# Issuing the wo loads of a layernorm, linear-attention and GEGLU block before the xn transposes

## The chip, the cores and the metric

The kernel runs on one core of a Trainium2 chip. The metric is device time in microseconds (us), the median of three runs. The profile is one further execution, read by engine: PE (matmuls; PEld is its weight load), ACT, DVE, POOL, and SP, which here only issues DMAs.

## The reference

One sequence of 2048 tokens, width 448, 16 heads of 28, hidden width 1792, all bf16.

```python
x = A_x
h = x + A(layernorm(x), wqkv, wo)
out = h + B(layernorm(h), w_gate, w_up, w_down)

# A: q, k, v = split(x @ wqkv);  phi(t) = where(t > 0, t + 1, exp(t)) + 1e-6
#    kv = phi(k)^T v;  z = sum(phi(k));  o = phi(q) kv / (phi(q) z + 1e-6);  return o @ wo
# B: (gelu(x @ w_gate) * (x @ w_up)) @ w_down
```

## The kernel before

The 2048 tokens are 16 tiles of 128. Three stages overlap. In the first, each tile of x is loaded, its statistics are taken (`bnst`, `bnag`), it is normalised into `xn` (`norm`), and it is transposed into `xnT`, so that the width lies on the partitions. Tiles 0 to 3 are transposed on PE (`tr0` to `tr3`). Tiles 4 to 15 are transposed by DMA: `xT4` to `xT15`, each a DMA_TRANSPOSE that SP issues (L526), once POOL has written `xn` of the tile and ACT has copied the last 64 columns beside it (`dup`). PE then computes K and V of each tile (`k4`, `v4` and so on: 14 matmuls from `xnT`, in two halves) and adds phi(K)^T V into two PSUM banks (`acc`). Q comes in four chunks of 512 tokens (`qa`, `qb`).

In the second stage PE forms numerator and denominator (`nd`), o is transposed (tiles 0 and 1 on PE, the others by `oT` DMA transposes), and `wo0` to `wo14b` multiply by `wo_sb`. In the third, h is normalised and transposed (`hT`), PE runs gate and up (`gu0` to `gu55`, from `wgu_sb`), ACT the gelu, DVE the product, and `down` multiplies by `wd_sb`.

The order on every engine is written out by hand: `ORDERS` holds one string of task names for each of PE, ACT, DVE, POOL and SP, and each engine runs its tasks strictly in that order, waiting on semaphores for what a task reads. A wait in SP's string therefore holds back every DMA behind it. All loads are issued by SP except the K and V weights, which ACT issues at the start.

`wo_sb` is filled by four DMAs: `dwo` and `dwo_s` of 128 x 3 rows of 448 elements (336 KB each), and `dwo_t` and `dwo_u` of 64 rows (56 KB each). They write parts of `wo_sb` that nothing else writes, and they read only the input. Three names near them matter below: `dwq`, `dwq_t`, `dwq_u` load the Q weights into `wq_sb`, `pqones` writes a 16 KB row of ones into `pqT`, and `dwg0` to `dwu6` load the gate and up weights into `wgu_sb` (14 DMAs of 224 KB).

Of the kernel before, what the change touches and what calls it, by code (L numbers as in the profile page):

```python
# [61 lines left out]
)  # L62
# [168 lines left out]
def bass_sequential_preLN__linear_attn_block__glu_gated_geglu__prompt_kernel(  # L231
    nc, A_x, A_wqkv, A_wo, B_x, B_w_gate, B_w_up, B_w_down, out, cfg=None
):
    cfg = dict(cfg or {})
    S, D, FF = 2048, 448, 1792
# [25 lines left out]
    with es:  # L261
        block = es.enter_context(nc.Block())

        def sb(name, shape, dt):
            return es.enter_context(nc.sbuf_tensor(name, shape, dt))
# [7 lines left out]
        wo_sb = sb("wo_sb", [128, 7, D], BF16)  # L273
# [41 lines left out]
        def bufs(name, n):  # L315
            return [_Buf("%s%d" % (name, i)) for i in range(n)]
# [4 lines left out]
        b_wk, b_wv, b_wq, b_wo = _Buf("wk"), _Buf("wv"), bufs("wq", 4), bufs("wo", 4)  # L321
# [38 lines left out]
        def dma(out_ap, in_ap, w, name, nbytes, q="sp", key=None, r=(), after=(), first=False):  # L360
            ik[0] += 0.01
            if first:
                after = chain[q][-1:]
            t_ = G.add(q, lambda e: e.dma_start(out_ap, in_ap), r=r, w=w, name=name, kind="dma", key=ik[0] if key is None else key, nbytes=nbytes, after=after)
            if first:
                chain[q].append(t_)
            return t_

        def op(eng, fn, r, w, name, dur, key=None, after=()):
            if key is None:  # L370
                ik[0] += 0.01
                key = ik[0]
            return G.add(eng, fn, r=r, w=w, name=name, dur=dur, key=key, after=after)
# [18 lines left out]
        dma(wq_sb[:, 0:3, 0:D], krows(A_wqkv, 0, 384, 0, D), [b_wq[0]], "dwq", 384 * D * 2, first=True)  # L392
        dma(wq_sb[0:64, 3, 0:D], A_wqkv[384:448, 0:D], [b_wq[1]], "dwq_t", 64 * D * 2, first=True)
        dma(wq_sb[64:128, 3, 0:D], A_wqkv[384:448, 0:D], [b_wq[2]], "dwq_u", 64 * D * 2, first=True)
        op("pool", lambda e: e.memset(ones_bf[:], 1.0), [], [b_ones], "ones", 0.20)  # L395
        op("pool", lambda e: e.affine_select(ident[:], ones_bf[:], [[1, 128]], ALU.is_equal, 0.0, base=0, channel_multiplier=-1),
           [b_ones], [b_ident], "ident", 0.30)
# [131 lines left out]
        wg3 = B_w_gate.rearrange("(k p) n -> p k n", p=64)  # L529
        wu3 = B_w_up.rearrange("(k p) n -> p k n", p=64)  # L530
        prev = xts[-1:]
        prev = [dma(wo_sb[:, 0:3, :], A_wo[0:384, :].rearrange("(g p) n -> p g n", p=128), [b_wo[0]], "dwo", 384 * D * 2, after=prev, key=19.0)]
        prev = [dma(wo_sb[0:64, 3, :], A_wo[384:448, :], [b_wo[1]], "dwo_t", 64 * D * 2, after=prev, key=19.0)]
        prev = [dma(wo_sb[64:128, 3, :], A_wo[0:64, :], [b_wo[2]], "dwo_u", 64 * D * 2, after=prev, key=19.0)]
        prev = [dma(wo_sb[:, 4:7, :], A_wo[64:448, :].rearrange("(g p) n -> p g n", p=128), [b_wo[3]], "dwo_s", 384 * D * 2, after=prev, key=19.0)]
        for k in range(7):
            prev = [dma(wgu_sb[0:64, k, :], wg3[:, k, :], [b_wg[k]], "dwg%d" % k, 64 * FF * 2, after=prev, key=20.0)]
            prev = [dma(wgu_sb[64:128, k, :], wu3[:, k, :], [b_wu[k]], "dwu%d" % k, 64 * FF * 2, after=prev, key=20.0)]
# [374 lines left out]
```

## Time and profile before

| | us |
|---|---|
| median of 3 runs | 196.42 (196.16 to 196.70) |
| profiled execution, its time | 196.7 |
| its span, first to last instruction | 194.9 |
| PE busy | 190.3 (98%) |
| PEld, DVE, ACT, POOL busy | 137.9, 116.3, 78.2, 42.0 |
| DMA traffic | 17.53 MB, mean 90 GB/s |

A row of the timeline reads: start, duration, engine, source line, operation, what is written and read, and how many. For a DMA on SP the duration is that of the issue; the time to landing stands in the list of DMA issues. Line 430 is a helper that issues most matmuls, and line 364 is the helper of all plain DMAs, so their rows are told apart by the tiles that they name. The span is 1.8 us shorter than the time of the same execution.

### The profile page before, as it was taken

How to read it: one execution, taken by the hardware profiler on the slowest of the kernel's cores; microseconds unless marked ns; L12 is line 12 of the kernel's file. 1: busy time of each engine (PE TensorE's matmuls, PEld its weight loads, DVE VectorE, ACT ScalarE, POOL GpSimd, SP SyncE). 2: the span in 40 equal slices, each digit the busy share in tenths (PEclk: the TensorE clock that was granted, in tenths of full speed). 3: DMA queues.
4: the chain of work that ended last, by engine and by line, in shares of the span. 5: the costliest groups of instructions: out<-in, count | busy, mean ns of one | idle time of the engine just before them, and what ended most of it. 6: DMA issues, size and time to landing. Idle time of an engine off the chain costs nothing.

```text
span 194.9 us, 5336 instructions
## 1 busy us (share of the span) xinstructions
PE 190.3 (98%) x2192; PEld 137.9 (71%) x2192; DVE 116.3 (60%) x301; ACT 78.2 (40%) x205; POOL 42.0 (22%) x90
## 2 busy tenths in 40 slices
PE   7999999999999999999999999999999999999994
PEld 7556658754588977976675577877778779899554
DVE  2989735368998946843967745756735443431512
ACT  3689866669784212220442441233232442411100
POOL 3099974300050310500500500500500000000000
PEclk9999999999999999999999999999999999999999
DMA  6944558999836052152062250172040000010111
GB/s 191 377 116 97 81 110 185 247 248 205 260 103 110 15 101 50 50 105 62 10 129 46 46 106 2 30 117 51 5 94 28 23 0 0 3 47 3 47 47 47
DMA packets 37256, 17.53 MB, mean 90 GB/s; under 512 B 28272, under 2 KB 36336, under 8 KB 37232
## 3 DMA queue, kind: packets, MB, share of 16 engines
q1 hardware_dynamic: 36352, 16.45, 36.8%
q10 hardware_dynamic: 880, 0.75, 1.2%
q8 instruction: 17, 0.28, 0.6%
q14 instruction: 7, 0.06, 0.1%
HBM read 8.72 MB, written 1.84 MB: 54 GB/s over the span
## 4 chain that ended last, share of the span: by engine, by line
PE 96%; issue 1%; ACT 1%; DVE 1%; POOL 0%; DVEq 0%; ACTq 0%; POOLq 0%
PE ps L430 87%; PE ps L780 6%; PE ps L454 2%; DVE x_sb L660 1%; PE ps L495 1%; ACT xn L617 1%; PE ps L681 0%; ACT xnT L523 0%; PE ps L672 0%; DVE x_sb L756 0%; POOL ones_bf L395 0%; POOL eps_t L398 0%; ACT pqT L616 0%; DVEq L196 0%; ACTq L196 0%
## 5 line engine op out<-in xcount | busy, mean ns | idle before, releaser
L430 PE MATMUL ps<-hnT,wgu_sb 64*128 64x512 bf16 (+1 forms) x980 | 90.4, 333 | 0.0
L430 PEld LDWEIGHTS ps<-hnT,wgu_sb 64*128 64x128 bf16 x980 | 64.5, 94 | 18.6 <-DVE hh L832 1.7
L830 ACT ACTIVATE gl<-ps 128x256 bf16<-128x256 f32 x112 | 36.9, 381 | 89.3 <-PE ps L430 88.2
L832 DVE TENSOR_TENSOR hh<-ps,gl 128x256 bf16<-128x256 f32 x112 | 42.5, 415 | 35.7 <-ACT gl L830 31.5
L430 PE MATMUL ps<-wd_sb,hh 64*128 64x448 bf16 x336 | 34.4, 349 | 0.0
L430 PEld LDWEIGHTS ps<-wd_sb,hh 64*128 64x128 bf16 x336 | 25.6, 94 | 6.2 <-DVE x_sb L756 0.2
L430 PE MATMUL ps<-wkv_sb,xnT 64*128 64x448 bf16 x192 | 22.4, 350 | 0.4 <-ACT xnT L523 0.4
L462 DVE BATCH_NORM_STATS2 st<-x_sb 128x6 f32<-128x448 bf16 x32 | 18.7, 611 | 2.6 <-DMA x_sb<-in_A_x_dram 2.6
L756 DVE TENSOR_TENSOR x_sb<-ps,x_sb 128x448 bf16<-128x448 f32 (+1 forms) x17 | 9.9, 591 | 16.6 <-PE ps L430 9.8
L474 POOL TENSOR_SCALAR ln<-mv 128x2 f32<-128x2 f32 x7 | 1.6, 223 | 75.0 <-DVE mv L463 74.9
L568 DVE SCALAR_TENSOR_TENSOR pk<-ps,tm 128x448 bf16<-128x448 f32 x16 | 9.8, 620 | 9.6 <-POOL tm L566 7.1
L430 PE MATMUL ps<-xnT,wq_sb 64*128 64x512 bf16 x112 | 14.9, 377 | 0.2 <-ACT xn L617 0.2
L430 PEld LDWEIGHTS ps<-wkv_sb,xnT 64*128 64x128 bf16 x192 | 10.1, 94 | 6.3 <-issue 0.8
L430 PE MATMUL ps<-wo_sb,oT 64*128 64x448 bf16 x98 | 12.1, 350 | 0.1
L660 DVE TENSOR_TENSOR x_sb<-ps,x_sb 128x448 bf16<-128x448 f32 x16 | 9.4, 618 | 4.6 <-PE ps L430 4.4
L780 PE MATMUL ps<-wd_sb,hh 128*128 128x448 bf16 (+1 forms) x70 | 10.8, 315 | 0.0
L566 POOL TENSOR_SCALAR tm<-e 128x448 bf16<-128x448 bf16 x16 | 8.9, 559 | 6.4 <-ACT e L565 5.5
L487 POOL TENSOR_SCALAR hn<-x_sb,nm,rs 128x448 bf16<-128x448 bf16 x14 | 10.0, 720 | 0.8 <-POOL rs L476 0.2
L565 ACT ACTIVATE e<-ps 128x448 bf16<-128x448 f32 x16 | 8.5, 541 | 3.5 <-PE ps L430 2.2
L780 PEld LDWEIGHTS ps<-wd_sb,hh 128*128 128x128 bf16 x70 | 6.7, 98 | 4.3 <-issue 0.4
L655 DVE TENSOR_TENSOR o_sb<-ps,rd 128x448 bf16<-128x448 f32 x16 | 9.4, 612 | 0.1
L570 ACT ACTIVATE v<-ps 128x448 bf16<-128x448 f32 x16 | 8.4, 542 | 2.1 <-PE ps L430 2.1
(69 smaller groups left out, 140.4 us busy)
## 6 DMA issues: line engine op xcount, KB each, us to landing
out_dram<-x_sb SPq DMA_DIRECT2D x15, 112.0 KB, 1.7
wgu_sb<-in_B_w_gate_dram SPq DMA_DIRECT2D x7, 224.0 KB, 6.1
wgu_sb<-in_B_w_up_dram SPq DMA_DIRECT2D x7, 224.0 KB, 6.4
wd_sb<-in_B_w_down_dram SPq DMA_DIRECT2D x1, 1568.0 KB, 8.3
x_sb<-in_A_x_dram SPq DMA_DIRECT2D x2, 448.0 KB, 5.3
wkv_sb<-in_A_wqkv_dram ACTq DMA_DIRECT2D x2, 336.0 KB, 3.7
x_sb<-in_A_x_dram SPq DMA_DIRECT2D x3, 224.0 KB, 4.2
wo_sb<-in_A_wo_dram SPq DMA_DIRECT2D x2, 336.0 KB, 4.4
```

The lines of the kernel that those rows point to most:

```text
L430: ins = e.matmul(o_, l_, r_, start=s_, stop=p_, **kw)
L462: op("dve", lambda e: e.bn_stats(st[:, t, :], src_ap), [b_src], [b_st[t]], "%sbnst%d" % ("" if mv is mv1 else "h", t), 0.53, key, after=after)
L487: return lambda e: e.tensor_scalar(dst, src[:, t, :], nm[:, t:t + 1], rs[:, t:t + 1], ALU.add, ALU.mult)
L565: act_exp(lambda e: e.activation(e1[:, ie, :], oK, AF.Exp), bank(bk), [b_e1[ie]], "ek%d" % t, _c_act(D), kk)
L566: op("pool", lambda e: e.tensor_scalar(tm1[:, ie, :], e1[:, ie, :], 1.0 + EPS, 0.0, ALU.min, ALU.max), [b_e1[ie]], [b_tm1[ie]], "cl%d" % t ...
L568: op("dve", lambda e: e.scalar_tensor_tensor(pk[:, i, :, 0:GW], psK3, EPS, tm1[:, ie, :].rearrange("p (g e) -> p g e", g=NG), ALU.max, ALU ...
L655: op("dve", lambda e: e.tensor_tensor(o_sb[:, so, oc:oc + D].rearrange("p (a e) -> p a e", e=28), nd3[:, :, 0:28], rd[:, i, :].unsqueeze(2 ...
L660: op("dve", lambda e: e.tensor_tensor(h_sb[:, u, :], ps[:, b, 0:D], x_sb[:, u, :], ALU.add), bank(b) + [b_x[u]], [b_h[u]], "hr%d" % u, 0.5 ...
L756: op("dve", lambda e: e.tensor_tensor(x_sb[:, t, c0:c1], ps[:, bk, c0:c1], h_sb[:, t, c0:c1], ALU.add), bank(bk) + [b_h[t]], [bo], "out%d% ...
L780: ins = e.matmul(ps[:, bk, c0:c1], hh[:, j, hsl(t)], wd_sb[:, j, c0:c1], start=(j == 0), stop=(j == NJ - 1))
L830: G.add("act", lambda e, gi=gi, cs_=cs_, psG=psG: e.activation(gl[:, gi, cs_], psG[:, cs_], AF.Gelu_apprx_tanh), r=bank(BK_G[i]), w=[b_glh ...
L832: op("dve", lambda e, dst=dst, srcU=srcU, srcL=srcL: e.tensor_tensor(dst, srcU, srcL, ALU.mult), bank(BK_U[i]) + [b_glh], [b_ar[j_][t % HR ...
```

## The change

The four wo loads move in SP's order from behind `xT15` to behind `dwq_u`, ahead of `pqones` and of `xT4`. They are chained to the first loads instead of to the transposes. No other engine's order changes.

```diff
-    "dx0 dx1 dx2 dwv_t dx4 dx6 dx8 dx12 dwq dwq_t dwq_u pqones xT4 xT5 ... xT15"
-    " dwo dwo_t dwo_u dwo_s dwg0 dwu0 ...
+    "dx0 dx1 dx2 dwv_t dx4 dx6 dx8 dx12 dwq dwq_t dwq_u dwo dwo_t dwo_u dwo_s pqones xT4 xT5 ... xT15"
+    " dwg0 dwu0 ...
...
         dma(wq_sb[64:128, 3, 0:D], A_wqkv[384:448, 0:D], [b_wq[2]], "dwq_u", 64 * D * 2, first=True)
+        dma(wo_sb[:, 0:3, :], A_wo[0:384, :].rearrange("(g p) n -> p g n", p=128), [b_wo[0]], "dwo", 384 * D * 2, first=True)
+        dma(wo_sb[0:64, 3, :], A_wo[384:448, :], [b_wo[1]], "dwo_t", 64 * D * 2, first=True)
+        dma(wo_sb[64:128, 3, :], A_wo[0:64, :], [b_wo[2]], "dwo_u", 64 * D * 2, first=True)
+        dma(wo_sb[:, 4:7, :], A_wo[64:448, :].rearrange("(g p) n -> p g n", p=128), [b_wo[3]], "dwo_s", 384 * D * 2, first=True)
...
         prev = xts[-1:]
-        prev = [dma(wo_sb[:, 0:3, :], ..., "dwo", 384 * D * 2, after=prev, key=19.0)]
-        prev = [dma(wo_sb[0:64, 3, :], ..., "dwo_t", 64 * D * 2, after=prev, key=19.0)]
-        prev = [dma(wo_sb[64:128, 3, :], ..., "dwo_u", 64 * D * 2, after=prev, key=19.0)]
-        prev = [dma(wo_sb[:, 4:7, :], ..., "dwo_s", 384 * D * 2, after=prev, key=19.0)]
```

On SP, from the Q weights to the first gate weights, the program before reads as follows (`wq_sb` are the Q weights, `pqT` the ones, `xnT` the twelve transposes, `wgu_sb` the gate and up weights):

```order
L364 DMA wq_sb<-in_A_wqkv_dram 128x3x448
L364 DMA wq_sb<-in_A_wqkv_dram 64x448 x2
L364 DMA pqT<-ones_bf 1x64x128
L526 DMA_TRANSPOSE xnT<-xn 128x4x128 x12
L364 DMA wo_sb<-in_A_wo_dram 128x3x448
L364 DMA wo_sb<-in_A_wo_dram 64x448 x2
L364 DMA wo_sb<-in_A_wo_dram 128x3x448
L364 DMA wgu_sb<-in_B_w_gate_dram 64x1792
```

The same stretch of SP in the changed program (its transposes stand four lines further down in the file):

```order
L364 DMA wq_sb<-in_A_wqkv_dram 128x3x448
L364 DMA wq_sb<-in_A_wqkv_dram 64x448 x2
L364 DMA wo_sb<-in_A_wo_dram 128x3x448
L364 DMA wo_sb<-in_A_wo_dram 64x448 x2
L364 DMA wo_sb<-in_A_wo_dram 128x3x448
L364 DMA pqT<-ones_bf 1x64x128
L530 DMA_TRANSPOSE xnT<-xn 128x4x128 x12
L364 DMA wgu_sb<-in_B_w_gate_dram 64x1792
```

The four wo loads now stand ahead of the ones and of all twelve transposes, and the first gate load follows the last transpose directly. From there on SP's order is the same as before.

More of the change, by code (lines that the diff above doesn't have):

```diff
@@ L531, in bass_sequential_preLN__linear_attn_block__glu_gated_geglu__prompt_kernel @@
         prev = xts[-1:]
[L532 to L535, printed above, removed]
         for k in range(7):
```

4 rows, old and new, of the table ORDERS are left out of this document.

## The prediction

> **What bounds the kernel now.** I read the chain that ended last first, then what PE waited for, then SP's timeline with the landings of its DMAs. From the page, the chain by engine; then three pieces of the chain in order of time; then the two waits of PE that lie behind the point to which wo moves:
>
> ```profile
> PE 96%; issue 1%; ACT 1%; DVE 1%; POOL 0%; DVEq 0%; ACTq 0%; POOLq 0%
> ...
> 10.51 27.04 PE ps L430 x336
> ...
> 62.84 40.46 PE ps L430 x552
> ...
> 103.35 78.37 PE ps L430 x776
> ...
> PE ps L430 <- DVE x_sb L660: 0.2, 1, 0.2
> PE ps L430 <- ACT xn L617: 0.2, 1, 0.2
> ```
>
> The chain is PE's own order for 96% of the span, in pieces of up to 78 us without a wait. So a change can gain only what PE waits for, and it loses whatever it makes PE wait. Late in the first 60 us PE waits twice, 0.2 us each, for DVE and for ACT, never for a DMA.
>
> When are the wo weights read? The first wo matmuls on PE's timeline, and the first of the second kind (from both halves of `wo_sb`), then the first gate and up matmuls:
>
> ```profile
> 47.02 0.74 PE L688 MATMUL ps<-wo_sb,oT 128*128 128x448 bf16 x3
> ...
> 50.07 0.94 PE L430 MATMUL ps<-wo_sb,oT 64*128 64x448 bf16 x8
> ...
> 54.13 0.60 PE L430 MATMUL ps<-hnT,wgu_sb 64*128 64x256 bf16 x8
> ```
>
> And when are they there? SP's timeline, start and issue time, with four landings between (us from issue to landing, from the list of issues of a short window: `dwo_s`, issued at 31.23, the last `wgu_sb` load, issued at 40.91, and the two `oT` transposes behind it):
>
> ```profile
> 28.64 3.19 SPq L364 DMA_DIRECT2D wo_sb<-in_A_wo_dram  x4
> wo_sb<-in_A_wo_dram SPq DMA_DIRECT2D x1, 336.0 KB, 4.9
> 31.87 0.50 SPq L364 DMA_DIRECT2D wgu_sb<-in_B_w_gate_dram  x1
> wgu_sb<-in_B_w_up_dram SPq DMA_DIRECT2D x1, 224.0 KB, 7.5
> 45.48 1.21 SPq L729 DMA_TRANSPOSE oT<-o_sb  x1
> oT<-o_sb SPq DMA_TRANSPOSE x1, 3.5
> oT<-o_sb SPq DMA_TRANSPOSE x1, 2.6
> ```
>
> The last piece of wo lands at 31.23 + 4.9 = 36.1, and PE reads it first at 47.0: 10.9 us to spare. The last gate or up piece lands at 40.91 + 7.5 = 48.4, and PE reads them first at 54.1: 5.7 us to spare. Nothing waits for either.
>
> **What it takes out.** The four issues leave the place behind `xT15`, so SP starts the gate and up loads 3.2 us earlier (31.87 - 28.64). What follows them, the first `oT`, has to wait for DVE in any case (SP stands from the last `wgu_sb` issue, about 41.5, until 45.48). The backlog of weights ahead of it is gone: that transpose landed 3.5 us after its issue, where the undisturbed ones take 2.5 (below), so it may land 1.0 us sooner, at 48.0. Its reader is the wo pair at 50.07, which stands in PE's order behind the Q matmuls that waited for ACT at 49.21. The second `oT`, issued at 46.7, landed at 46.7 + 2.6 = 49.3, also in time. The gain is 0, and at most the two waits above, 0.2 + 0.2 = 0.4 us.
>
> **What it adds on SP.** Rows of SP's timeline where the loads go:
>
> ```profile
> 4.98 1.86 SPq L364 DMA_DIRECT2D wq_sb<-in_A_wqkv_dram  x3
> 6.88 0.60 SPq L364 DMA_DIRECT2D pqT<-ones_bf  x1
> pqT<-ones_bf SPq DMA_DIRECT2D x1, 16.0 KB, 5.3
> 11.65 1.30 SPq L526 DMA_TRANSPOSE xnT<-xn  x1
> xnT<-xn SPq DMA_TRANSPOSE x1, 2.5
> ```
>
> Four issues at the pace of the Q loads (1.86 / 3 = 0.62) are 2.5 us, and at the pace of the wo issues themselves 3.2. SP stands idle from 7.48 to 11.65, since `xT4` waits for its tile of `xn`. So `pqones` is issued at 9.4 to 10.1 and done by 10.7 at the latest, and `xT4` still goes out at 11.65. Cost 0. That cover is 1.0 to 1.7 us; beyond it, every us would delay all twelve transposes. `pqones` itself is read by the `nd` matmuls after 41 us.
>
> **What it adds on the DMA engines.** This is the only place where the change can hurt: 784 KB (0.803 MB) now stand in the same queue ahead of `xT4`. Two rows by stretches of 1 us before the loads run dry, and three after it (last column GB/s, the one before it the DMA share), and the engine's instruction traffic from the list of queues in the window 10.5 to 11:
>
> ```profile
> 5.00:6.00 1.00, 1.00 (x11) 0.90 (x9) 0.84 (x5) 0.50 (x2) 0.00 (x0) 1.00 1.10 374
> 9.00:10.00 1.00, 1.00 (x20) 0.58 (x16) 0.95 (x3) 0.80 (x3) 0.35 (x2) 1.00 1.09 379
> 10.00:11.00 1.00, 1.00 (x22) 0.52 (x22) 0.57 (x2) 1.00 (x4) 0.77 (x2) 1.00 0.88 266
> 11.00:12.00 1.00, 1.00 (x16) 0.61 (x16) 1.00 (x5) 1.00 (x4) 1.00 (x2) 1.00 0.00 0
> 12.00:13.00 1.00, 1.00 (x14) 0.49 (x10) 1.00 (x4) 0.92 (x5) 1.00 (x4) 1.00 0.03 6
> q8 instruction: 1, 0.02, 15.7%
> ```
>
> The queue is full at 374 to 379 GB/s and runs dry at about 10.7 (266 of 377 is 0.7 of that slice). Then it is empty for two us, until the first bytes of `xT4` near 12.95. At 377 GB/s wo takes 0.803 / 377 = 2.13 us and ends near 12.85. It fits into the hole almost exactly.
>
> Two things can push it over the edge. One instruction load (the q8 row: 15.7% of 16 engines x 0.5 us = 1.26 us of one engine) falls at the end of that queue; one of the sixteen may be up to 1.26 us late. And a transpose right behind copies lands late: the `oT` issued at 45.48 landed at 49.0, 0.6 us after the last weights ahead of it (48.4). In the new order `pqones` is what stands ahead; it landed at 6.88 + 5.3 = 12.2 and would land 2.13 later, at 14.3, so `xT4` lands at 14.3 + 0.6 = 14.9 instead of 11.65 + 2.5 = 14.15. The ends are 14.15 (no delay) and 14.9 + 1.26 = 16.2; I take 14.9, since the `oT` row is the same kind of transition, and since the landing of `pqones` already contains part of the instruction load.
>
> The Trainium skill, "DMA: Bandwidth & Descriptors", section "Queues, rings and completion order", speaks against this change: on each engine the descriptors of one issuing queue are consumed in ring order, so `xT4` has to stand behind wo. The trace agrees: the `oT` behind the weights took 3.5 us and not 2.5. The same page, section "Bandwidth", gives 341 GB/s for a 1 MB load; by that, as an estimate, wo would take 2.35 us and everything here would be 0.2 later.
>
> **When PE needs it.** The weight load of `k4` and of what follows:
>
> ```profile
> 15.30 0.09 PEld L430 LDWEIGHTS ps<-wkv_sb,xnT 64*128 64x128 bf16 x1
> ...
> 16.55 0.90 PEld L430 LDWEIGHTS ps<-wkv_sb,xnT 64*128 64x128 bf16 x12
> 13.06 1.20 SPq L526 DMA_TRANSPOSE xnT<-xn  x1
> ```
>
> `k4` begins at 15.30: 1.15 us after `xT4` landed before, 0.4 us after 14.9. `xT5`, issued at 13.06, lands at 15.6, for a `k5` that begins half way through the twelve loads from 16.55, near 17.0: 1.4 us to spare, and no more than what `xT4` has left of it. So `k4` alone decides, and in the sum it does not wait.
>
> **The sum.** Gain 0, SP 0, DMA 0.75 us of `xT4`'s slack and 0 us of PE: 196.7 stays 196.7 in the profiled execution, which is the slowest of the three runs; 196.4 in terms of the median. About 0.3% (0.6 us) is what a measurement of this kernel can tell from no change.
>
> **Rivals.** *Slower: `xT4` lands after 15.30.* From there each us is a us of PE, with no wait behind to give it back but the 0.4 above. What decides is whether wo runs at the pace of the early loads or at that of the later ones:
>
> ```profile
> 30.00:32.00 2.00, 2.00 (x25) 1.98 (x22) 1.08 (x3) 0.75 (x2) 1.19 (x2) 1.00 0.65 176
> 32.00:34.00 2.00, 2.00 (x28) 1.28 (x25) 0.95 (x2) 1.87 (x4) 0.98 (x2) 1.00 0.91 251
> ```
>
> These are the stretches in which wo itself moved. At 251 GB/s it takes 3.2 us, 1.07 more, `xT4` lands at 16.0, and PE stands 0.7 us: 197.1, or +0.35%. With the late engine in full on top, 17.2 and 1.9 us: 198.3. Against it: in that place wo was held up by its issues, and it shared the stretch with 64-partition gate loads; the Q loads, of the same row length, sit in the full-speed stretch. The late engine alone gives 16.2 and 0.9 us: 197.3.
>
> *Faster: the earlier gate and up loads and `oT` reach PE.* The price is at most 0.4 us: 196.0, under 0.3% even so. Against it: both waits are for ACT and DVE. For a gain beyond 0.6 us I find no wait that could go.
>
> *The loads move, but their data does not come earlier* (the queue stands, SP is held up). Nothing reads wo before 47, so the time is again 196.4, unless SP is held past 11.65; that is the slower rival by another way.
>
> **How the numbers follow.** No change within 0.3%: 0.60, the sum and the inert case together. Slower by more: 0.33, since the sum leaves only 0.4 us where the bounds of the two unknown terms reach 0.9 to 1.9 over; the point is `xT4` landing at 15.9. Faster by more: 0.07, for what the views do not show. The predicted time is 196.4. The range goes from 196.4 - 0.6 = 195.8, the edge of no change, to 198.0, just under the end of the slower rival.
>
> **What would show it.** SP's timeline: four `wo_sb` issues between 6.9 and 10.1, the first transpose still at 11.65, the first gate load near 28.6. DMA by stretches: about 377 GB/s until 12.85 and no hole. `xT4` lands near 14.9; the weight load at 15.30 stays where it is. Wrong if PE shows a wait before the `k4` weights, or if the first transpose's issue moves.

## The result and the profile after

The changed kernel takes 197.09 us (median of 9 runs, 196.68 to 197.43), the kernel before 196.42 (9 runs, 196.16 to 196.71). The ratio is 1.0034, 95% interval 1.0024 to 1.0044: slower by 0.67 us. The time lies in the range, but the likeliest case, no change, was wrong; it went as the slower rival.

SP's timeline of the changed kernel where wo now stands:

```profile
7.07 2.40 SPq L364 DMA_DIRECT2D wo_sb<-in_A_wo_dram  x4
9.51 0.59 SPq L364 DMA_DIRECT2D pqT<-ones_bf  x1
11.20 2.10 SPq L530 DMA_TRANSPOSE xnT<-xn  x1
```

And from the list of DMA issues, us from issue to landing: the last of the four, `dwo_s`, issued at 8.88; the ones (`pqones`); `xT4`:

```profile
wo_sb<-in_A_wo_dram SPq DMA_DIRECT2D x1, 336.0 KB, 6.4
...
pqT<-ones_bf SPq DMA_DIRECT2D x1, 16.0 KB, 6.1
...
xnT<-xn SPq DMA_TRANSPOSE x1, 4.7
```

The issues fit into SP's idle time as forecast. The landings do not: `dwo_s` 15.3, the ones 15.6, `xT4` 11.20 + 4.7 = 15.9, where 14.9 was forecast. PE's timeline at `k4` and at the two later waits, first before:

```profile
15.52 0.79 PE L430 MATMUL ps<-wkv_sb,xnT 64*128 64x448 bf16 x6
...
49.21 1.04 PE L430 MATMUL ps<-xnT,wq_sb 64*128 64x512 bf16 x8 [0.19 <-ACT xn L617]
...
53.47 0.82 PE L430 MATMUL ps<-kvz,pqT 49*128 49x116 bf16 x15 [0.21 <-DVE x_sb L660]
```

and in the changed kernel:

```profile
14.41 0.82 PE L434 MATMUL ps<-xnT,wq_sb 64*128 64x512 bf16 x6
15.98 0.74 PE L434 MATMUL ps<-wkv_sb,xnT 64*128 64x448 bf16 x6 [0.75 <-ACT e L625]
...
49.55 1.04 PE L434 MATMUL ps<-xnT,wq_sb 64*128 64x512 bf16 x8 [0.19 <-ACT xn L617]
...
53.82 0.82 PE L434 MATMUL ps<-kvz,pqT 49*128 49x116 bf16 x15 [0.21 <-DVE x_sb L660]
```

The longest piece of the chain of waits, which started at 103.35 before:

```profile
103.69 78.38 PE ps L434 x776
```

`k4` starts at 15.98, 0.1 us after `xT4` landed, and PE stood 0.75 us. The row names ACT (L625), one of whose instructions happens to end then. `k4` does not wait for that one: in the profile of before it began at 15.72, after `k4`. That it is the DMA is what the experiments test. In this execution `k0` ran 0.46 us earlier than in the profile shown of before (6.97, not 7.43), so `k4` is only 0.46 us later than there. Behind it the same places stand 0.34 (49.55 and 103.69) and 0.35 us (53.82) later than before: 0.1 of the 0.46 us is given back. The two later waits are as long as before, to the hundredth.

By stretches of 1 us (last columns: clock, DMA share, GB/s):

```profile
12.00:13.00 1.00, 1.00 (x14) 0.54 (x12) 1.00 (x4) 0.50 (x3) 1.00 (x3) 1.00 1.04 323
13.00:14.00 1.00, 1.00 (x14) 0.46 (x12) 1.00 (x4) 1.00 (x4) 1.00 (x3) 1.00 1.75 185
14.00:15.00 1.00, 1.00 (x18) 0.48 (x14) 0.87 (x4) 1.00 (x4) 1.00 (x3) 1.00 0.61 33
```

The bulk of wo is through at 13, as forecast. But between 14 and 15, with `xT4` and `xT5` issued and PE about to need the first, the DMA engines move 33 GB/s, less than a tenth of the 377 at which they ran from 9 to 10. Something waits for a rest.

The single packets in the traces tell what. In the profile of before, 512 packets of 256 bytes move between 12.9 and 13.8, and beside them only some of 4 bytes: that is `xT4`. In the changed kernel 517 packets of under 512 bytes move between 12.9 and 13.7 (the ones, 64 packets, are among them), so most of `xT4` had been moved by then. What was left of wo came from 13.9 to 14.7 at 2 or 3 packets of 896 bytes per 0.1 us, the pace of one engine (41 ns each). And the others stood: 24 packets that began between 13.58 and 14.69 ended together, at 15.07 to 15.10. (That is why the DMA share of 13 to 14 is 1.75: it counts the whole time of a packet where the packet begins.) All 16 counts of the semaphore of `dwo_s` came behind that, from 15.10 to 15.27. So the landings at 15.3 and 15.6 tell when this stand ended, and not when the data had moved.

### The profile page after: what moved, and what is told of

Read it like the earlier page. It is cut to its first block, busy times and chain, and to the rows that moved or that the text cites. A ratio compares the mean times of both kernels' runs of the same rounds, so it can differ in the third digit from the quotient of the medians.

```text
span 195.3 us, 5336 instructions
## 1 busy us (share of the span) xinstructions
PE 189.7 (97%) x2192; PEld 136.5 (70%) x2192; DVE 116.3 (60%) x301; ACT 78.7 (40%) x205; POOL 42.2 (22%) x90
## 4 chain that ended last, share of the span: by engine, by line
PE 92%; ACT 2%; DMA 2%; DVE 1%; issue 1%; SPq 0%; DVEq 0%; ACTq 0%
PE ps L434 85%; PE ps L780 6%; DMA x_sb<-in_A_x_dram 2%; DVE x_sb L660 1%; ACT xn L617 1%; PE ps L499 1%; ACT e L565 1%; ACT v L570 0%; PE ps L681 0%; DVE st L466 0%; PE ps L672 0%; ACT e L625 0%; ACT ln L471 0%; DVE xn L490 0%; DVE x_sb L756 0%
## 5 line engine op out<-in xcount | busy, mean ns | idle before, releaser
L434 PE MATMUL ps<-xnT,wq_sb 64*128 64x512 bf16 x112 | 14.9, 377 | 0.2 <-ACT xn L617 0.2
L434 PE MATMUL ps<-wo_sb,oT 64*128 64x448 bf16 x98 | 12.1, 349 | 0.1
```

The source lines that it names most:

```text
L434: ins = e.matmul(o_, l_, r_, start=s_, stop=p_, **kw)
```

## The experiments

Three theories. A: `xT4` stands in its queue behind the wo data, and PE waits for it. B: the issues on SP cost. C: the far end costs, where the gate and up loads now come earlier. Later A was split: A1, the transpose waits for the slowest DMA engine; A2, it waits for the bytes. For A1 the counts of the semaphores are needed: in these traces the semaphore of a load gets 16 counts, which I read as one from each engine, and the load has landed with the last.

What they gave, with the landing of `xT4` (issue plus time to landing) and PE's wait in front of `k4`, each from the one profiled execution, and the times as ratio to the kernel before, run beside each group (its medians are 196.42 to 196.60), with a 95% interval:

| loads ahead of `xT4` | `xT4` lands | PE waits | median us | ratio |
|---|---|---|---|---|
| none (before) | 14.2 | 0 | 196.42 | |
| wo, 784 KB (changed) | 15.9 | 0.75 | 197.09 | 1.0034 (1.0024 to 1.0044) |
| three wo loads, 448 KB | 14.7 | 0 | 196.54 | 1.0002 (0.9993 to 1.0010) |
| a copy of wo, 784 KB | 16.4 | 0.89 | 197.39 | 1.0049 (1.0033 to 1.0064) |
| none; wo ahead of `xT11` | 14.3 | 0 | 196.53 | 1.0014 (0.9999 to 1.0030) |
| wo and 448 KB gate/up | 19.0 | 3.37 | 200.64 | 1.0194 (1.0158 to 1.0229) |
| wo and 448 KB of 128-partition rows | 17.3 | 2.16 | 199.48 | 1.0139 (1.0109 to 1.0170) |
| wo; instruction load later | 16.0 | 0.39 | 197.66 | 1.0048 (1.0034 to 1.0061) |
| none; instruction load later | 14.8 | 0 | 197.07 | 1.0024 (1.0010 to 1.0038) |
| wo; instruction load sooner | 16.5 | 1.05 | 197.67 | 1.0043 (1.0030 to 1.0056) |
| 448 KB and 61 rows | 15.3 | 0.33 | 196.83 | 1.0015 (1.0006 to 1.0024) |
| 448 KB and 64 rows | 15.7 | 0.27 | 196.69 | 1.0007 (0.9997 to 1.0017) |
| 448 KB and 127 rows | 18.3 | 2.87 | 201.11 | 1.0220 (1.0187 to 1.0253) |
| 448 KB and 128 rows | 15.2 | 0 | 196.59 | 1.0005 (0.9997 to 1.0014) |

In two rows the profiled execution is not like the median: with wo ahead of `xT11` it was the slowest of twelve (197.79), and with no wo and the instruction load later nearly the fastest of twelve (196.47), so its landing and wait do not explain that row's 197.07.

**Part of the change alone.** Three loads early, the fourth at its old place:

```diff
-    "... dwq_u dwo dwo_t dwo_u dwo_s pqones xT4 ...    ... xT15 dwg0 ..."
+    "... dwq_u dwo dwo_t dwo_u pqones xT4 ...    ... xT15 dwo_s dwg0 ..."
```

> Three of the four wo loads (dwo, dwo_t, dwo_u, 448 KB) stand ahead of xT4, and dwo_s stays behind xT15. Theory A (the queue): xT4 stands in its ring behind the wo data and k4 waits for it; with 336 KB less ahead it lands 336 KB / 377 GB/s = 0.9 us sooner than in the changed kernel, near 14.95, so nearly all of the loss goes: 196.4 to 196.6. Theory B (the issues on SP): what costs is the four issues and the longer issue of xT4; three of four remain, so three quarters of the loss: 196.9. Theory C (the far end): wo gone from behind xT15 is what costs, by the gate and up loads that come earlier; half of it is undone: 196.75.

Measured 196.54, no loss. `k4` starts at 15.30 without a wait, `xT4` having landed at 14.7. That is A; B and C expected 0.3 us or more.

**The early half alone.** The wo loads stay, and a second copy goes to an unread tile `wo2_sb`:

```diff
+        dma(wo2_sb[:, 0:3, :], A_wo[0:384, :]..., "dxo", ...)   # and dxo_t, dxo_u, dxo_s like it
+    "... dwq_u dxo dxo_t dxo_u dxo_s pqones xT4 ... xT15 dwo dwo_t dwo_u dwo_s dwg0 ..."
```

> The kernel before, with a second copy of the four wo loads, into a tile that nobody reads, issued ahead of xT4; the wo loads that are read stay behind xT15. Only the early half of the change. Theory A: as the changed kernel, 197.1, with xT4 landing near 15.85 and k4 waiting for it. Theory B: 197.1 too. Theory C: 196.4, since the far end is as before.

Measured 197.39. The far end is that of before, and the loss is there: C falls. The issue of `xT4` took 1.31 us here, as in the kernel before, so the 2.10 us that it took in the changed kernel are not what makes it land late.

**The late half alone.** wo ahead of `xT11`, so that the gate and up loads follow `xT15` as in the changed kernel:

```diff
+    "... xT10 dwo dwo_t dwo_u dwo_s xT11 xT12 xT13 xT14 xT15 dwg0 ..."
```

> All four wo loads leave their old place, but stand between xT10 and xT11, whose tile PE reads near 29.7, and not ahead of xT4. The far end is as in the changed kernel. Theory A: xT4 lands at 14.2 as before, xT11 and those behind it have 3 to 5 us to spare before and use up to 3 of them: 196.4. Theory B: five transposes are issued 2.5 to 3.2 us later, without a reader that waits: 196.4. Theory C: 197.1, since the gate and up loads start as early as in the changed kernel.

Measured 196.53, as A expected; but the interval only just takes in 1. Nine of the twelve times lie between 196.16 and 196.71, three between 197.38 and 197.79, and the profiled execution, the slowest, shows why. `xT11`, issued at 24.57, landed 5.1 us later, and PE's timeline has

```profile
29.76 0.85 PE L430 MATMUL ps<-wkv_sb,xnT 64*128 64x448 bf16 x6 [0.31 <-DMA xnT<-xn]
31.61 0.74 PE L430 MATMUL ps<-wkv_sb,xnT 64*128 64x448 bf16 x6 [0.81 <-DMA xnT<-xn]
```

Three to five us to spare are eaten there by the same 784 KB. So there, too, the transposes behind wo can pay for it.

**More of it.** 448 KB more ahead of `xT4`, first as the gate and up pieces of 64 partitions each, later as rows for 128 partitions:

```diff
+    "... dwo_s dwg0 dwu0 pqones xT4 ..."      # 64 partitions each
+    "... dwo_s dwx pqones xT4 ..."            # 512 rows of w_down into an unread tile
```

> The changed kernel with two more loads ahead of xT4, the first gate and up pieces (448 KB). Theory A: 448 KB / 377 GB/s = 1.2 us more in the queue, xT4 lands near 17.05 and PE waits 1.2 us more: 198.3. Theory B: two issues of 0.6 us more fit into SP's idle time before xT4, at most 0.2 us: 197.1 to 197.3. Theory C: 197.1.

> The changed kernel with 448 KB more ahead of xT4, as in the run with the two gate and up pieces, but as rows for all 128 partitions (512 rows of the down weights into a tile that nobody reads; the down weights still load later). If the bytes set the delay: 1.2 us more than the changed kernel, xT4 at 17.05, 198.3. If the shape of 64 partitions made no difference there: as that run, xT4 near 18.9, 200.6.

Here the trace names the DMA outright. PE in front of `k4`, first with the gate and up pieces, then with the rows:

```profile
19.06 0.74 PE L438 MATMUL ps<-wkv_sb,xnT 64*128 64x448 bf16 x6 [3.37 <-DMA xnT<-xn]
```

```profile
17.38 0.99 PE L436 MATMUL ps<-wkv_sb,xnT 64*128 64x448 bf16 x6 [2.16 <-DMA xnT<-xn]
```

As rows, `xT4` lands at 17.3, near the 17.05 of 1.2 us for the bytes; as 64-partition pieces at 19.0, 1.7 us later for the same bytes. So in these two executions the shape counts. B, which expected 197.1 to 197.3, falls. Both medians are above the sum of 198.3, in part because the clock fell behind the wait in four of the six executions and in two of the four (last section). In the others the times are 198.88 and 199.73 with the pieces, 198.31 and 198.92 with the rows.

**Is it one late engine?** In the changed kernel the semaphore of `dwo` gets its 15th of 16 counts at 13.14 and the last at 14.02: one engine is 0.9 us behind. In that stretch one engine also serves an instruction load of PE. I moved that load by changing the number of warm-up matmuls:

```diff
-    ins = e.matmul(ps[:, 0, 0:128], ones_bf[:], ones_bf[:], ...)      # x38
+    ins = e.matmul(ps[:, 0, :], ones_bf[:], wide, ...)                # later: x11 of 512 columns
+    ins = e.matmul(ps[:, 0, 0:64], ones_bf[:], ones_bf[:, 0:64], ...) # sooner: x76 of 64 columns
```

(For the later load, the 16 narrower warm-up matmuls also became 4.)

> The changed kernel, with the 54 warm-up matmuls at the start of PE made into 15 wider ones: 78 instructions fewer, about the same time on PE. PE's instruction load that fell on one DMA engine at 11.76, in the middle of the wo data, should come about 2.6 us later, near 14.3. Theory A1 (the late engine): that load is what makes one engine late and so the landing of dwo_s and of xT4; without it there dwo_s lands near 14.2 and xT4 near 14.7, k4 does not wait: 196.4 to 196.6. Theory A2 (the bytes and the change from copies to transposes alone): the load does not matter, xT4 lands near 15.8: 197.1.

> The kernel before with the same 15 warm-up matmuls, as the control of the last one. Theory A1: the instruction load moves from the end of the x and Q loads to about 13.4, onto xT4 or xT5; if it hits xT4, that lands up to 1.3 us later, at 15.5, and k4 waits up to 0.2: 196.4 to 196.7. Theory A2: 196.45.

> The changed kernel with the 38 warm-up matmuls of 128 columns made into 76 of 64: 76 instructions more, so the instruction load should come about 2.5 us sooner, near 9.2, still inside the full queue. Theory A1: an engine that has fallen behind in a full queue stays behind until the queue runs dry, so nothing is gained: 197.1, xT4 near 15.8. If only a load at the very end of the queue hurts: 196.5. Theory A2: 197.1.

The first of these missed: 197.66. The load came at 13.28, not 14.3, still inside the queue, where it hit `dwo_s` instead of `dwo`. And its control lost as well, 197.07 (expected 196.4 to 196.7). So the times of this pair decide nothing. The landings say more. Without the load in its stretch `dwo_u` was complete at 13.58, not 14.37. And with the load sooner, its row in the window 8.8 to 8.95 (42.0% of 16 engines x 0.15 us, 1.0 us of one engine):

```profile
q8 instruction: 1, 0.02, 42.0%
```

The x tiles complete just before have their 15th and 16th count at 9.04 and 9.09; the next ones at 10.29 and 11.77, and `dwo_u` at 13.43 and 15.07. One engine fell 1.5 us behind at the load and stayed there until the queue ran dry; `xT4` landed at 16.5.

**One late engine made to order.** Three wo loads early, no loss, and behind them rows of 896 bytes into an unread tile:

```diff
+        dma(wz_sb[0:61, :], A_wo[0:61, :], [b_wz], "dwz", 61 * D * 2, first=True)   # also 64, 127, 128 rows
+    "... dwo dwo_t dwo_u dwz pqones xT4 ..."
```

> The kernel with three wo loads early (448 KB, no loss), and a load of 61 rows of 896 bytes (55 KB, into a tile that nobody needs) behind them, ahead of xT4. The Trainium skill, DMA: Bandwidth & Descriptors, section Why a DMA increments its semaphore by 16 and not by 1: a load of 61 rows runs on one engine, 64 rows on all 16. Sentences without it: if these rows go over all engines, they take 0.15 us, and the time stays 196.6. Theory A1 (the transposes wait for the slowest engine): if they go to one engine, 61 packets of some 41 ns make it 2.5 us late, at about 15.3, xT4 lands near 16.1, 1.3 us later than with three loads alone, and k4 waits about 1 us: 197.4. Theory A2 (bytes alone): 196.6 either way, since it is 55 KB.

> The control of the last run: 64 rows (57 KB) in place of 61. Theories A1 and A2 alike: spread over all engines, 0.15 us more, xT4 near 14.9, no wait or 0.1 us: 196.6.

61 rows gave 196.83, not 197.4, and do not stand apart from 64 rows: that engine's lateness probably ran beside the other's and hardly exceeded it. Inconclusive; so twice as much:

> As the run with 61 rows, with 127 rows of 896 bytes (114 KB). Those 61 went to one engine (their semaphore got one late count, at 14.83), but they ran beside another engine that was late already, so the two could not be told apart. 127 packets of some 41 ns make that engine 5.2 us late, far beyond the other. Theory A1 (a transpose lands only when the slowest engine is through): the load lands at 14.83 + 66 x 0.041 = 17.5, xT4 0.5 us later at 18.0, PE waits 2.7 to 3.1 us: 199.3 to 199.7. Theory A2 (the bytes in the queue): 114 KB are 0.3 us, xT4 at 15.0 to 15.9: 196.6 to 197.1.

> The control: 128 rows (115 KB), which go to all 16 engines. Both theories: 0.3 us more in the queue than with three wo loads alone, xT4 at 15.0 to 15.9, 196.6 to 197.1.

This is the plainest pair: 111 KB and 112 KB, 201.11 and 196.59 us. (Of the six executions with 127 rows one kept its full clock; it took 199.13, near the 199.3 to 199.7 that A1 expected.) The semaphore of the 127 rows gets 2 counts, the last at 17.65, where that of 128 rows gets 16: they ran on one engine, as the Trainium skill says, "DMA: Bandwidth & Descriptors", "Why a DMA increments its semaphore by 16 and not by 1". `xT4` lands at 18.3. By stretches (the second number is PE's busy time, the last two DMA share and GB/s), with 127 rows:

```profile
15.00:16.00 1.00, 0.54 (x6) 0.04 (x2) 1.00 (x3) 1.00 (x4) 1.00 (x3) 1.00 3.89 45
16.00:17.00 1.00, 0.00 (x0) 0.00 (x0) 1.00 (x4) 0.95 (x4) 1.00 (x2) 1.00 0.07 23
```

PE's timeline of the same run:

```profile
18.40 0.74 PE L436 MATMUL ps<-wkv_sb,xnT 64*128 64x448 bf16 x6 [2.87 <-DMA xnT<-xn]
```

With 128 rows, the stretch and then PE's timeline:

```profile
15.00:16.00 1.00, 1.00 (x13) 0.56 (x10) 1.00 (x3) 1.00 (x4) 1.00 (x2) 1.00 0.63 122
```

```profile
15.52 0.80 PE L436 MATMUL ps<-wkv_sb,xnT 64*128 64x448 bf16 x6
```

From 15 to 17 PE stands, and the DMA moves 45 and 23 GB/s: one engine of sixteen at work, with `xT4` issued at 12.97 and waiting for it. Nearly all of `xT4` had been moved: 498 packets of under 512 bytes between 14.4 and 15.2, and 23 from there to 17.1. (SP was itself held in the issue of the ones, 3.21 us, so `xT4` went out 1.3 us late; that explains landing at 15.5, not at 18.3.) A1 holds, A2 falls.

What no run shows is the changed kernel without an instruction load among the wo data: the run that was to show it only moved the load to another place in the same queue.

## Why the prediction was wrong

The steps, in its order:

- *Bound and gain.* Right. The gate and up loads are issued by 39.3 instead of 41.5 (2.2 us sooner; 3.2 was forecast), the first `oT` lands 2.4 us after its issue instead of 3.5, as forecast, and PE's two later waits are unchanged: the gain is 0.
- *SP.* Right: four issues in 2.40 us, done at 10.1, `xT4` not held back. It went out at 11.20, but its issue took 2.10 us.
- *The bytes.* Right: the bulk of wo is through at 13, where 12.85 was forecast, at 323 to 339 GB/s from 10 on, where 377 was.
- *The landing of `xT4`.* Here it failed. The step "I take 14.9 ... since the landing of `pqones` already contains part of the instruction load" took the late engine as paid for. The step from copies to transposes was no dearer than taken (`xT4` followed the ones by 0.2 us, where 0.6 was taken), but the ones landed at 15.6, not 14.3. In the old queue the load fell when the queue was nearly dry, so the engine had little left to be late with; in the new one it began at 11.76 with some 1.3 us of wo still to move, and the engine was late with its part of that to the end. The term measured 0.7 to 0.9 us (15th against 16th count of `dwo_u`, 13.65 and 14.37, and of `dwo`), beside 0.3 us by which the Q loads ahead were later in this execution (the last complete at 12.1, not 11.8; by the 15th count 0.15 us). The term lay inside the bound of 1.26 that the prediction carried, and the sum set it to nothing.
- *`k4` decides.* Right, and with it the slower rival: "the late engine alone gives 16.2 and 0.9 us: 197.3". Measured: `xT4` at 15.9, PE's wait 0.75, 197.09. The rival's other half, wo at 251 GB/s, was not needed. The slack was off as well: PE was free for `k4` at 15.23 in this execution (14.41 + 0.82), not at 15.52 as in the profile before, whose execution was the slowest of its three. So of the 0.4 us of slack some 0.3 hung on the execution that was profiled. The rival had the landing 0.3 us too late and `k4` 0.3 us too late, so that its 197.3 came so near is partly luck.

The chance that this rival got, 0.33, was too small for a margin of 0.4 us beneath a bound of 1.3 us. What remains open: why one engine was already some tenths behind before the load in several of the runs, whether the loss goes when that load falls elsewhere, and how much of the loss of the control with 15 warm-up matmuls is the load hitting a transpose.

## What to carry to other kernels

A load put into idle time is hidden only if whatever is queued behind it can wait for its slowest engine, and not merely for its bytes. Before a load moves ahead of a DMA transpose, compare the slack of that transpose's reader with the bytes at full rate plus one instruction load of one engine (0.9 to 1.3 us in these runs); that the bytes fit on the average is not enough. Half of this change, the three loads of 448 KB, cost nothing; the last 336 KB went over the edge.

## What the runs showed of the hardware

A transpose in a queue behind copies landed 0.2 to 0.5 us after the last count of these copies, in every run in which it had to wait, and it did not help it that the other engines were through with their share. They were held as well: with the 127 rows, packets that began between 15.0 and 15.9 ended at 17.5 to 17.6, behind the late engine's part of the transpose.

A load of 127 rows of 896 bytes went to one engine and took to 17.65; 128 rows went to all and were complete by 14.7.

A wait of PE of 2 to 3 us can cost more than its length. With the 448 KB of rows, PE stood 2.16 us, and the granted clock behind it (third number from the right) was

```profile
17.38:18.00 0.62, 0.62 (x6) 0.41 (x8) 0.62 (x2) 0.00 (x0) 0.48 (x3) 0.79 1.25 247
18.00:19.00 1.00, 1.00 (x15) 0.67 (x12) 0.44 (x1) 0.00 (x0) 0.00 (x0) 0.50 0.43 87
...
20.00:21.00 1.00, 1.00 (x8) 0.55 (x6) 0.00 (x0) 0.71 (x2) 0.09 (x1) 0.50 0.58 117
21.00:22.00 1.00, 1.00 (x18) 0.59 (x16) 0.49 (x1) 0.74 (x4) 1.00 (x2) 0.92 0.00 0
```

half speed for some 3.4 us. It did not fall in every execution: the mean clock of the whole execution was 0.991 in two of four with these rows, in four of six with the gate and up pieces and in five of six with the 127 rows, and 1.00 in the others. The waits of 0.27 to 1.05 us in the other runs left it at 1.00. The Trainium skill, "TensorE: Matmul & The Clock Gate", "Part 1: The HAM clock gate (the "warmup" mystery)", names an idle window of about 3.4 us for this; the wait of 3.37 us with the gate and up pieces fits, but 2.16 was enough here.
